# Attention and two feed-forward layers on one core: two score tiles in place of one, and late units' v product joined to later scores

## The chip, the cores and the metric

One core of one Trainium2 chip runs the whole program. The metric is the device time of one execution in microseconds, the median of several runs.

## What is computed

```python
def _attn_ref(q, k, v):                     # B, H, S, D = 4, 8, 576, 64
    scores = scale * np.matmul(q, k.transpose(0, 1, 3, 2))
    mask = block_i >= block_j               # blocks of 64 positions
    scores = np.where(mask, scores, -1000000000.0)
    attn = np.exp(scores - np.max(scores, axis=-1, keepdims=True))
    attn = attn / (np.sum(attn, axis=-1, keepdims=True) + 1e-09)
    return np.matmul(attn, v)
...                                         # heads side by side: x is 2304 x 512
    h = x @ w_in                            # 512 x 2048
    g = np.maximum(h, 0.0) + np.log1p(np.exp(-np.abs(h)))
    x = g @ w_out                           # 2048 x 512
...
    h = x @ w_in                            # second layer, 512 x 1024
    solu = h * softmax(h)
    out = (layer_norm(solu) * g_ln) @ w_out # 1024 x 512
```

Matrix products are made of float32 operands split in a high and a low part; a product is three matmuls.

## The kernel before

All work is recorded first as tasks in a `Plan`: an engine, a cost, the tasks it waits for, and a rank. The ranks are tables of numbers written at the top (`RANK` by group, `OFF` by kind of task). The planner makes from them one order for each engine, the kernel is emitted in that order, and each engine then runs its instructions in that order. Between engines the framework adds semaphore waits, by tile: it knows that a tile was written or read, and of neighbouring accesses of one engine to the same tile it signals the last.

The stages overlap. Their names here:

- **A units** (`UnitA`, n = 0 to 15): the first 256 queries of four batches, two heads at a time. Scores on TensorE (`mm_qk`), mask, maximum, scale and denominators on VectorE, exp on ScalarE, product with v (`pv`) on TensorE, then the rows of x (`x_hi`, `x_lo`) into `xt`. Units 8 to 15, the late ones, normalise on VectorE (`norm`), split (`split`), transpose by DMA (`tr_dma`), and `merge` into `psA`. Their scores take the PSUM tile `r`, from unit 12 on `r` and `R` in turn. `pv` writes into columns 0 to 255 of the unit's own tile, and the next unit on the same tile waits until `x_lo` has read it.
- **Pieces** (32): conversions of the first layer's weights, four steps on VectorE and one on ScalarE each, of 512 KB loads into `raw`; results are `w` and `w2w`.
- **Pairs** (72): 256 tokens and two 128-column slices of the first layer. On TensorE 24 matmuls `hp<-xt,w` (two *a blocks* of 12), then exp and ln on ScalarE, `t`, `gh`, `gl` on VectorE, and 24 matmuls `acc<-gh,w` and `acc<-gl,w` (two *b blocks* of 12). A chunk of tokens can start when its x is complete.
- **C units** (`UnitC`, 16): queries 256 to 575. TensorE: `mm_both` writes scores of blocks 0 (two heads, 384 columns) and 1 (two heads, 512 columns), 12 matmuls without a break; after a few a and b blocks the scores of block 2 (`mm_qk(2)`, 6 matmuls, written `S<-qkh` with 128x288 in the trace), which reuse the banks of block 0; and `pv` of the unit before (`S<-ps,v` and `S<-p,v`). VectorE: `mask` for blocks 0 and 1 (L467), `max` (L472) for 0, 1 and later 2. ScalarE: `exp` (L481), two heads of block 0 (`exp0`), two of block 1 (`exp1`), one instruction for block 2 (`exp2`). Then split, DMA transposes, merges into `ps` (L522), and `scale` (L538) and x from `pv`'s result.
- After the last C unit's x: the second layer, in which TensorE runs without gaps.

All four banks of a C unit's scores are one tile, `state["S"]` (L821): block 0 in banks 0 and 1, block 1 in banks 2 and 3, block 2 in banks 0 and 1 again, `pv` in bank 3 (`BANKS`, L76).

Of the kernel before, what the change touches and what calls it, by code (L numbers as in the profile page):

```python
# [10 lines left out]
F32 = mybir.dt.float32  # L11
# [12 lines left out]
    "Pair.a": -354.9, "Pair.abs": 39459.0, "Pair.b": 18236.7, "Pair.do_gh": 216226.0, "Pair.do_gl": 13257.7,  # L24
    "Pair.evac": -82948.2, "Pair.exp": -117702.0, "Pair.ln": -30665.3, "Pair.store": -79781.5, "Pair.stt": -62739.8,
    "Piece.bits0": -100434.0, "Piece.bits0@P0": -27714.9, "Piece.bits1": 65312.7, "Piece.bits1@P0": -101077.0,
    "Piece.do_hi": -19168.6, "Piece.do_hi@P0": -29991.6, "Piece.do_hi_g": -10835.1, "Piece.do_lo": 62401.8,
    "Piece.do_lo@P": -122217.0, "Piece.do_lo@P0": -16882.1, "Piece.do_lo_g": -33281.2, "Piece.load": 61438.7,
    "Piece.load@P0": -221951.0, "Piece.signed": -4876.1, "Piece.signed@P0": -103215.0, "Tok.a": -132718.0,
    "Tok.aggr": 7517.3, "Tok.bm": 58620.7, "Tok.center": -11408.7, "Tok.exp": -45235.8, "Tok.ln_hi": 28283.8,  # L30
    "Tok.ln_lo": 116041.0, "Tok.load": -268344.0, "Tok.logexp": -134098.0, "Tok.max": -65917.9,
    "Tok.merge": -135054.0, "Tok.mul": 52834.8, "Tok.o_evac": 47450.1, "Tok.small1": 71861.5, "Tok.small2": -55930.6,
    "Tok.split": -4685.6, "Tok.split_hi": 24778.5, "Tok.split_lo": -127140.0, "Tok.stats": 68934.5,
    "Tok.store": 157613.0, "Tok.tr": -45442.3, "Tok.x_hi": -107660.0, "Tok.x_lo": -20156.8, "UnitA.copy": -193390.0,
# [15 lines left out]
    "UnitC.den2": 65738.1, "UnitC.exp": 104667.0, "UnitC.load_qk": -83707.0, "UnitC.load_v": -36917.0,  # L50
    "UnitC.mask": -89564.7, "UnitC.max": -78960.5, "UnitC.merge": 54501.7, "UnitC.merge4": 149992.0,
    "UnitC.mm_both": -120396.0, "UnitC.mm_qk": -21356.3, "UnitC.norm": 76221.3, "UnitC.pv": -31503.3,
    "UnitC.qk_hi": -189467.0, "UnitC.qk_lo": -5389.2, "UnitC.rs_load": 138338.0, "UnitC.rs_store": -59470.7,
    "UnitC.scale": -44805.3, "UnitC.split": 94027.7, "UnitC.tr": -223984.0, "UnitC.x_hi": 131467.0,
    "UnitC.x_lo": 10651.6, "UnitC.xx": -154207.0,
}
RANK = {
# [3 lines left out]
    "Tok": (611105.0, 4133.14),  # L61
# [14 lines left out]
BANKS = (slice(0, 2), slice(2, 4), slice(0, 2))  # L76
# [139 lines left out]
def dve_ns(n, per=1.04):  # L216
    return 70.0 + per * n
# [11 lines left out]
def body(ctx: ExitStack, tc: tile.TileContext, qk, qkA, vP, vA, w1, w2, u1, u2, gln, out):  # L229
# [127 lines left out]
    class UnitC:  # L357
# [6 lines left out]
        def plan(self, prev, opened):  # L364
# [10 lines left out]
            for i, w in enumerate(WC):  # L375
# [10 lines left out]
                if i == 1 and p1:  # L386
                    p1.tail([self.t_exp[1, 1]])
# [58 lines left out]
        def scores(self, i):  # L446

            return state["S"][:, BANKS[i], 0:WC[i] if i < 2 else WC[2] // 2]

# [98 lines left out]
    class UnitA:  # L548
# [6 lines left out]
        def plan(self, prev, rank, opened):  # L555
# [14 lines left out]
            self.t_mqk = add("PE", 760, rank, self.mm_qk, [self.t_qk] + free)  # L570
# [127 lines left out]
        def x_hi(self, e):  # L698
            copy(e, xt_of(self.b)[:, 0, self.pr, :], self.o)
# [453 lines left out]
```

## Time and profile before

| | us |
|---|---|
| median of 3 runs | 783.55 |
| lowest, highest | 781.19, 784.84 |
| profiled execution, own time | 784.22 |
| its span on the core | 782.4 |
| TensorE busy | 735.1 (94%) |
| VectorE busy | 592.7 (76%) |
| ScalarE busy | 409.8 (52%) |

The span runs from the first to the last instruction; 1.8 us of the execution lie outside it. The page gives engines as PE (TensorE), PEld (its weight loads), DVE (VectorE), ACT (ScalarE), SP (which issues the DMAs). Idle time in brackets stands ahead of the instruction on whose line it is, with the instruction that ended it. PEclk is the granted TensorE clock, 1.00 being 2.4 GHz and 0.5 being 1.2 GHz; a stretch's figure is a mean.

### The profile page before, as it was taken

Reading aid. Unit: us, or ns where it says so; the run is one execution under the profiler, and the core shown is the slowest. Engines: PE = TensorE matmul, PEld = TensorE weight load, DVE = VectorE, ACT = ScalarE, POOL = GpSimd, SP = SyncE. Lnnn points to the kernel's source line nnn. Section 1 sums busy time; section 2 is a strip of 40 time slices with the busy share of each in tenths; the row PEclk is TensorE's granted clock in tenths of the full one; section 3 lists DMA queues with packets and bytes.
Section 4 is the critical chain, followed back from the end, with each engine's and each line's share of the span. In section 5 each row is a group of like instructions: output and inputs, shape, how many; then the busy total and the mean of one; then the engine's idle time right before and its main releaser. Section 6 shows DMA issues by size and latency. Waiting matters only on the chain.

```text
span 782.4 us, 13713 instructions
## 1 busy us (share of the span) xinstructions
PE 735.1 (94%) x5288; PEld 652.5 (83%) x5288; DVE 592.7 (76%) x1232; ACT 409.8 (52%) x877; POOL 0.7 (0%) x6
## 2 busy tenths in 40 slices
PE   7899999999898988898898899999999999999998
PEld 4688989999877777777887699999999888888887
DVE  6899995565777876777888755634698998989883
ACT  5787855563765666655665645543454342233231
POOL 0000000000000000000000000000000000000000
PEclk9899999999999998999999999999999999999999
DMA  7665742223666665566876552302513524443233
GB/s 258 197 196 182 227 149 68 69 42 88 138 135 148 138 165 123 116 132 134 172 148 132 101 138 81 124 13 72 200 52 82 141 76 108 95 108 88 59 83 80
DMA packets 165216, 95.00 MB, mean 121 GB/s; under 512 B 134816, under 2 KB 148384, under 8 KB 165152
## 3 DMA queue, kind: packets, MB, share of 16 engines
q1 hardware_dynamic: 165152, 94.14, 47.9%
q8 instruction: 41, 0.67, 0.3%
q14 instruction: 23, 0.19, 0.1%
HBM read 51.91 MB, written 9.70 MB: 79 GB/s over the span
## 4 chain that ended last, share of the span: by engine, by line
PE 64%; DVE 18%; ACT 10%; DMA 4%; issue 3%; SPq 0%; ACTq 0%; DVEq 0%
PE hp L238 14%; PE acc L238 13%; PE op L238 13%; PE h L238 13%; PE S L238 8%; ACT eC L481 5%; DVE mC L472 4%; DMA raw<-in_w_dram 3%; PE R L238 2%; DVE ps L522 2%; DVE a L315 1%; DVE t L769 1%; DVE mA L627 1%; PE r L238 1%; ACT eA L636 1%
## 5 line engine op out<-in xcount | busy, mean ns | idle before, releaser
L238 PE MATMUL hp<-xt,w 128*128 128x256 f32 x1728 | 216.6, 282 | 0.4 <-DVE t L769 0.3
L238 PEld LDWEIGHTS hp<-xt,w 128*128 128x128 f32 x1728 | 207.7, 190 | 6.9 <-issue 5.2
L238 PE MATMUL acc<-gh,w 128*128 128x256 f32 x768 | 144.8, 281 | 0.5 <-ACT gh L244 0.5
L238 PEld LDWEIGHTS acc<-gh,w 128*128 128x128 f32 x768 | 121.4, 189 | 3.0 <-issue 2.1
L238 PE MATMUL acc<-gl,w 128*128 128x256 f32 x384 | 107.6, 280 | 1.8 <-DVE gl L777 1.7
L238 PE MATMUL h<-u,w 128*128 128x512 f32 x432 | 100.2, 389 | 0.0
L238 PE MATMUL op<-w,w2w 128*128 128x512 f32 (+1 forms) x456 | 100.0, 378 | 0.0
L238 PEld LDWEIGHTS op<-w,w2w 128*128 128x128 f32 x456 | 82.5, 188 | 16.0
L238 PEld LDWEIGHTS h<-u,w 128*128 128x128 f32 x432 | 80.8, 188 | 16.6
L481 ACT ACTIVATE eC<-S,mC 128x384 f32<-128x384 f32 (+2 forms) x80 | 52.0, 653 | 61.0 <-DVE mC L472 26.9
L760 ACT ACTIVATE t<-hp 128x512 f32<-128x512 f32 x72 | 42.7, 593 | 66.1 <-PE hp L238 55.6
L769 DVE SCALAR_TENSOR_TENSOR t<-hp,t 128x512 f32<-128x512 f32 x72 | 49.1, 682 | 35.9 <-ACT t L766 35.5
L238 PEld LDWEIGHTS acc<-gl,w 128*128 128x128 f32 x384 | 72.1, 188 | 2.5 <-DVE gl L777 2.4
L238 PE MATMUL S<-ps,v 128*64 128x320 f32 (+1 forms) x256 | 38.8, 450 | 14.9 <-ACT eC L481 12.9
L1070 ACT ACTIVATE ob<-op,A 128x512 f32<-128x512 f32 (+1 forms) x19 | 12.6, 663 | 75.8 <-PE op L238 72.8
L777 DVE TENSOR_TENSOR gl<-t,gh 128x512 fp32r<-128x512 f32 x72 | 49.3, 684 | 2.0 <-ACT gh L244 0.7
L472 DVE TENSOR_REDUCE mC<-S 128x2 f32<-128x768 f32 (+2 forms) x48 | 45.4, 974 | 6.3 <-ACT eC L481 3.7
L238 PE MATMUL acc<-gh,w2w 128*128 128x256 f32 x256 | 48.4, 281 | 0.0
L766 ACT ACTIVATE t<-t 128x512 f32<-128x512 f32 x72 | 45.5, 632 | 1.4
L763 ACT ACTIVATE t<-t 128x512 f32<-128x512 f32 x72 | 45.6, 633 | 1.2
L522 DVE COPY ps<-eC 128x1536 uint16<-128x1536 uint16 (+2 forms) x48 | 45.2, 945 | 1.4 <-DMA eC<-hl 1.3
L238 PEld LDWEIGHTS S<-ps,v 128*64 128x64 f32 x256 | 18.5, 149 | 32.5 <-ACT eC L481 14.5
(175 smaller groups left out, 1086.0 us busy)
## 6 DMA issues: line engine op xcount, KB each, us to landing
raw<-in_w_dram SPq DMA_DIRECT2D x32, 512.0 KB, 4.7
qkC<-in_qk_dram SPq DMA_DIRECT2D x16, 480.0 KB
raw_u<-in_u_dram SPq DMA_DIRECT2D x11, 512.0 KB, 3.5
v<-in_vP_dram SPq DMA_DIRECT2D x16, 320.0 KB, 2.9
x2s<-stg SPq DMA_DIRECT2D x18, 256.0 KB, 2.8
xr<-x2s SPq DMA_DIRECT2D x18, 256.0 KB, 3.2
qkA<-in_qkA_dram SPq DMA_DIRECT2D x16, 256.0 KB, 4.0
out_dram<-ob SPq DMA_DIRECT2D x15, 256.0 KB, 2.2
```

The lines of the kernel that those rows point to most:

```text
L238: PE.matmul(out, lhsT, rhs, start=start, stop=stop, skip_group_check=True)
L315: DVE.scalar_tensor_tensor(out=self.a, in0=self.raw[:, :, 0], scalar=29, in1=self.a, op0=ALU.logical_shift_right, op1=ALU.bitwise_or)
L472: DVE.tensor_reduce(out=self.m[:, i:4:2] if i < 2 else self.m[:, 4:5], in_=self.scores(i), axis=AX.X if i < 2 else AX.XY, op=ALU.max, nega ...
L481: ACT.activation(e, sc, AF.Exp, bias=self.m[:, c:c + 1], accum_out=self.den[:, d:d + 1])
L522: DVE.tensor_copy(dst, src)
L627: DVE.tensor_reduce(out=self.m[:, i, w * j:w * j + w], in_=st[:, :, QA[i]], axis=AX.X, op=ALU.max, negate=True)
L760: ACT.activation(self.t, self.hp, AF.Abs)
L763: ACT.activation(self.t, self.t, AF.Exp, scale=-1.0)
L766: ACT.activation(self.t, self.t, AF.Ln, bias=1.0)
L769: DVE.scalar_tensor_tensor(out=self.t, in0=self.hp, scalar=0.0, in1=self.t, op0=ALU.max, op1=ALU.add)
L777: DVE.tensor_sub(self.gl, self.t, self.gh)
L1070: ACT.activation(self.ob[:, cols], self.o[cols.start][:, cols], AF.Copy, scale=self.A)
```

## The change

Three things change.

First, `state["S"]` becomes a list of two tiles of two banks. Blocks 0 and 2 go to the first, block 1 and `pv` to the second. The instructions of a C unit stay the same in kind and size. `pv` of the unit before is planned after the second `exp1` instead of the first.

Second, late A units all use `r`. Their `pv` writes 6 matmuls of 128 columns into columns 384 to 511 of both halves of `r`, where it was 4 matmuls of 256 and 128 columns into columns 0 to 255, so scores of a later unit and this product stand side by side. From unit 10 on one task (`mm_pv`) makes unit n's scores and, right behind, unit n-2's `pv`; units 14 and 15 get a `pv` of their own. Scores from unit 9 on wait for the exp of the unit before in place of the `x_lo`; `pv` waits for the `x_lo` of the unit before.

Third, every number of `OFF` and `RANK` is another.

```diff
 OFF = {
-    "Pair.a": -354.9, "Pair.abs": 39459.0, "Pair.b": 18236.7, "Pair.do_gh": 216226.0, "Pair.do_gl": 13257.7,
+    "Pair.a": -17732.7, "Pair.abs": -25663.4, "Pair.b": 30817.0, "Pair.do_gh": 252422.0, "Pair.do_gl": 4374.1,
...
-BANKS = (slice(0, 2), slice(2, 4), slice(0, 2))
...
-                    p1.tail([self.t_exp[1, 1]])
+                    p1.tail([self.t_exp[1, 0]])
...
-            return state["S"][:, BANKS[i], 0:WC[i] if i < 2 else WC[2] // 2]
+            return state["S"][i % 2][:, :, 0:WC[i] if i < 2 else WC[2] // 2]
...
-            o, ps = state["S"][:, 3], state["ps"]
+            o, ps = state["S"][1][:, 1], state["ps"]
...
-            self.bank = ("R", "r", "acc", "hp")[n] if n < 4 else "r" if n in (8, 9, 10, 11) else ("r", "R")[n % 2]
-            free = [u.t_xl for u in prev if u.bank == self.bank][-1:]
-            if n >= 12 and self.bank == "R":
-                free += evacs[1]
+            self.bank = ("R", "r", "acc", "hp")[n] if n < 4 else "r" if n >= 8 else ("r", "R")[n % 2]
+            free = [u.t_xl for u in prev if u.bank == self.bank][-1:] if n < 9 else [p1.t_exp]
...
-            self.t_mqk = add("PE", 760, rank, self.mm_qk, [self.t_qk] + free)
+            if n >= 10:
+                self.t_mqk = p2.tail(add("PE", 760 + 760, rank, partial(self.mm_pv, p2), [self.t_qk] + free + p2.pv_deps()))
+            else:
+                self.t_mqk = add("PE", 760, rank, self.mm_qk, [self.t_qk] + free)
...
+        def pv_deps(self):
+            return [self.t_cp, self.t_v] + ([self.p1.t_xl] if self.n > 8 else [])
...
+        def mm_pv(self, p2):
+            self.mm_qk()
+            p2.pv()
+
         def pv(self):
+            if self.n >= 8:
+
+                self.o = state["r"][:, :, 384:512]
+                for x, t in ((0, 0), (1, 0), (1, 1)):
+                    for j in range(2):
+                        mm(self.o[64 * j:64 * j + 64, x], self.v[:, j, t, :], self.ps[:, j, 128 * (x + t):128 * (x + t) + 128], t == 0, x == t)
+                return
...
-        state["S"] = q.tile([128, 4, 512], F32, name="S")
+        state["S"] = [q.tile([128, 2, 512], F32, name=f"S{i}") for i in range(2)]
...
+    for n in (14, 15):
+        plan.at_group("A3", n % 4)
+        unitsA[n].tail(add("PE", 760, 0.0, unitsA[n].pv, unitsA[n].pv_deps()))
```

What moves on the engines is shown at four places. ScalarE in a late C unit, before (eC_2322, eC_2323 and eC_2324 are blocks 0, 1 and 2, hl their splits; `waits` names the engines waited for):

```order
448 L481 ACTIVATE eC_2322,dC_2318<-S,mC 128x384 [waits DMAHW4_49,DVE_49,PE_49]
449 L766 ACTIVATE t<-t 128x512 [waits Activation_49]
450 L481 ACTIVATE eC_2322,dC_2318<-S,mC 128x384
451 L481 ACTIVATE eC_2323,dC_2318<-S,mC 128x512 [waits DMAHW5_49]
452 L244 ACTIVATE hl_2325<-eC_2322 128x768 [waits Activation_49]
453 L481 ACTIVATE eC_2323,dC_2318<-S,mC 128x512 [waits PE_49]
454 L430 ACTIVATE qkh<-qkC 128x384 [waits DMAHW7_49]
455 L431 ACTIVATE qkh<-qkC 128x576
456 L244 ACTIVATE hl_2326<-eC_2323 128x1024 [waits Activation_49]
457 L481 ACTIVATE eC_2324,dC_2318<-S,mC 128x576 [waits DMAHW0_49,DVE_49,PE_49]
458 L760 ACTIVATE t<-hp_131 128x512
```

And in the changed kernel, at the corresponding unit (S_2008 and S_2009 are the two tiles, eC_2016 to eC_2018 the blocks):

```order
435 L480 ACTIVATE eC_2016,dC_2012<-S_2008,mC 128x384 [waits DMAHW2_49,DVE_49,PE_49]
436 L480 ACTIVATE eC_2016,dC_2012<-S_2008,mC 128x384
437 L480 ACTIVATE eC_2017,dC_2012<-S_2009,mC 128x512 [waits DMAHW3_49,DVE_49,PE_49]
438 L786 ACTIVATE t<-hp_131 128x512 [waits PE_49,Activation_49]
439 L480 ACTIVATE eC_2017,dC_2012<-S_2009,mC 128x512
440 L789 ACTIVATE t<-t 128x512 [waits Activation_49]
441 L429 ACTIVATE qkh<-qkC 128x384 [waits DMAHW4_49,PE_49]
442 L430 ACTIVATE qkh<-qkC 128x576
443 L792 ACTIVATE t<-t 128x512 [waits Activation_49]
444 L480 ACTIVATE eC_2018,dC_2012<-S_2008,mC 128x576 [waits DVE_49]
```

The order of the five exps is the same, but which one waits for TensorE is not: the second exp of block 1 and the exp of block 2 did, where the change has waits at the first exp of each tile, and none on TensorE at block 2.

TensorE at two late A units (qkA scores, vA the product, r and R the PSUM tiles), before:

```order
414 L238 MATMUL r<-psA,vA 64x256 x2
415 L238 MATMUL r<-psA,vA 64x128 x2
416 L238 MATMUL hp_131<-xt,w_7_104 128x256 x12
417 L238 MATMUL hp_130<-xt,w_8_105 128x256 x12
418 L238 MATMUL r<-qkA 128x128 x2
419 L238 MATMUL r<-qkA 128x256 x2
420 L238 MATMUL R<-psA,vA 64x256 x2
421 L238 MATMUL R<-psA,vA 64x128 x2
422 L238 MATMUL hp_130<-xt,w_9_106 128x256 x12
```

And after the change, where scores of a unit are followed at once by the product of the unit two before:

```order
300 L237 MATMUL hp_131<-xt,w_10_107 128x256 x12
301 L237 MATMUL hp_131<-xt,w_11_108 128x256 x12
302 L237 MATMUL r<-qkA 128x128 x2
303 L237 MATMUL r<-qkA 128x256 x2
304 L237 MATMUL r<-psA,vA 64x128 x6
305 L237 MATMUL hp_130<-xt,w_12_109 128x256 x12
306 L237 MATMUL hp_130<-xt,w_13_110 128x256 x12
307 L237 MATMUL hp_131<-xt,w_14_111 128x256 x12
```

The products stood alone, with their own wait for `psA`; now a scores task carries them, and all are in `r`.

VectorE where the last piece of `w2w` is made, before (a and w2w belong to pieces, mA, dA, eA and psA to late A units, t, gh, gl to pairs):

```order
234 L315 SCALAR_TENSOR_TENSOR a<-raw,a 128x512
235 L246 CAST w2w_126<-a 128x512
236 L325 TENSOR_TENSOR w2w_126<-a,w2w_126 128x512
237 L703 TENSOR_TENSOR xt<-r,xt 128x256
238 L769 SCALAR_TENSOR_TENSOR t<-hp_130,t 128x512
239 L246 CAST gh<-t 128x512
240 L777 TENSOR_TENSOR gl<-t,gh 128x512
241 L622 MEMSET r 64x4x64
242 L627 TENSOR_REDUCE mA<-r 128x2 x2
243 L769 SCALAR_TENSOR_TENSOR t<-hp_131,t 128x512
244 L630 TENSOR_SCALAR mA<-mA 128x4
```

And after the change:

```order
264 L652 TENSOR_SCALAR dA<-dA 128x4
265 L324 TENSOR_TENSOR w2w_126<-a,w2w_126 128x512
266 L655 RECIPROCAL dA<-dA 128x4
267 L660 TENSOR_SCALAR eA_147<-eA_147,dA 128x128 x2
268 L660 TENSOR_SCALAR eA_147<-eA_147,dA 128x256 x2
269 L245 COPY eA_149<-eA_147 128x768 x2
270 L795 SCALAR_TENSOR_TENSOR t<-hp_130,t 128x512
271 L245 CAST gh<-t 128x512
272 L803 TENSOR_TENSOR gl<-t,gh 128x512
273 L634 MEMSET r 64x4x64
274 L245 CAST xt<-r 128x256
275 L639 TENSOR_REDUCE mA<-r 128x2
```

Five late units still have their mask (MEMSET of r or R) and maxima behind the last piece before, two after the change: three more late units are ahead of it. In TensorE's order the first blocks that use each piece keep nearly the same place (w_15 behind 48 blocks of 12 matmuls, the second half of w2w behind 56, in both). The first `mm_both` of the C units stands behind 94 blocks before, 72 after the change; between it and the last `pv` stand 110 blocks before, 118 after.

SP, which issues the loads in this order, at the start before (qkA and vA are A units' inputs, raw the pieces'):

```order
1 L599 DMA qkA<-in_qkA_dram 128x512
2 L603 DMA vA<-in_vA_dram 128x256
3 L599 DMA qkA<-in_qkA_dram 128x512
4 L603 DMA vA<-in_vA_dram 128x256
5 L304 DMA raw<-in_w_dram 128x1024
6 L599 DMA qkA<-in_qkA_dram 128x512
7 L603 DMA vA<-in_vA_dram 128x256
8 L304 DMA raw<-in_w_dram 128x1024 x3
9 L599 DMA qkA<-in_qkA_dram 128x512
```

And after the change:

```order
1 L611 DMA qkA<-in_qkA_dram 128x512
2 L615 DMA vA<-in_vA_dram 128x256
3 L303 DMA raw<-in_w_dram 128x1024
4 L611 DMA qkA<-in_qkA_dram 128x512
5 L615 DMA vA<-in_vA_dram 128x256
6 L303 DMA raw<-in_w_dram 128x1024 x3
7 L611 DMA qkA<-in_qkA_dram 128x512
8 L615 DMA vA<-in_vA_dram 128x256
9 L611 DMA qkA<-in_qkA_dram 128x512
```

Four loads of raw now stand ahead of the third unit's qkA, where one did; raw has a limited number of buffers, and a load that has to wait for one holds those behind it.

## Rows read from the trace of the kernel before

**Rows 1.** The page, part 1: busy us, share of the span, instructions.

```profile
PE 735.1 (94%) x5288; PEld 652.5 (83%) x5288; DVE 592.7 (76%) x1232; ACT 409.8 (52%) x877; POOL 0.7 (0%) x6
```

**Rows 2.** Busy time by stretch: its length, then each engine; then PEclk, DMA.

```profile
34.00:116.00 82.00, 77.72 (x670) 72.75 (x672) 79.23 (x177) 61.31 (x135) 0.00 (x0) 1.00 0.61 193
180.00:464.00 284.00, 254.09 (x2001) 220.88 (x2000) 214.39 (x439) 170.16 (x373) 0.00 (x0) 0.97 0.62 135
280.00:300.00 20.00, 15.65 (x116) 14.20 (x112) 14.81 (x30) 13.23 (x30) 0.00 (x0) 0.87 0.65 148
```

**Rows 3.** Waits, 180 to 464 us: who for what, total, times, longest.

```profile
PE S L238 <- ACT eC L481: 27.5, 17, 4.0
ACT eC L481 <- DVE mC L472: 26.9, 17, 4.9
...
PE S L238 <- DVE mC L472: 1.9, 4, 1.1
```

**Rows 4.** TensorE timeline, C stage: start, us, operation, [idle before <-releaser].

```profile
199.27 0.53 PE L238 MATMUL S<-qkh 128*128 128x288 f32 x2 [1.41 <-ACT eC L481]
...
296.01 0.85 PE L238 MATMUL S<-qkh 128*128 128x288 f32 x2 [4.00 <-ACT eC L481]
...
312.62 0.53 PE L238 MATMUL S<-qkh 128*128 128x288 f32 x2 [0.47 <-ACT eC L481]
...
404.09 2.88 PE L238 MATMUL hp<-xt,w 128*128 128x256 f32 x24
...
415.17 0.53 PE L238 MATMUL S<-qkh 128*128 128x288 f32 x2 [2.34 <-ACT eC L481]
...
417.89 2.16 PE L238 MATMUL S<-ps,v 128*64 128x320 f32 x16 [0.28 <-DVE mC L472]
...
448.79 2.16 PE L238 MATMUL S<-ps,v 128*64 128x320 f32 x16 [1.59 <-ACT eC L481]
```

**Rows 5.** ScalarE timeline of the unit at 407 to 424 us.

```profile
412.70 0.58 ACT L481 ACTIVATE eC<-S,mC 128x384 f32<-128x384 f32 x1 [1.29 <-DVE mC L472]
...
416.26 0.69 ACT L481 ACTIVATE eC<-S,mC 128x512 f32<-128x512 f32 x1 [0.41 <-PE S L238]
...
420.45 0.74 ACT L481 ACTIVATE eC<-S,mC 128x576 f32<-128x576 f32 x1 [1.48 <-PE S L238]
```

**Rows 6.** VectorE timeline of the same unit.

```profile
410.53 2.09 DVE L472 TENSOR_REDUCE mC<-S 128x2 f32<-128x768 f32 x2
...
417.07 0.76 DVE L472 TENSOR_REDUCE mC<-S 128x1 f32<-128x576 f32 x1 [0.45 <-ACT eC L481]
```

**Rows 7.** Groups by shape, VectorE, 180-464 us: busy, mean ns | idle.

```profile
L472 DVE TENSOR_REDUCE mC<-S 128x2 f32<-128x1024 f32 x16 | 19.4, 1212 | 0.0
```

**Rows 8.** Groups by shape, VectorE, 34 to 130 us.

```profile
L627 DVE TENSOR_REDUCE mA<-r 128x2 f32<-128x512 f32 x5 | 3.4, 676 | 0.0
L246 DVE CAST w<-a 128x512 fp32r<-128x512 f32 x8 | 3.3, 415 | 0.1
...
L661 DVE COPY psA<-eA 128x1536 uint16<-128x1536 uint16 x3 | 2.9, 956 | 0.6 <-DMA eA<-eA 0.6
...
L648 DVE TENSOR_SCALAR eA<-eA,dA 128x256 f32<-128x256 f32 x8 | 2.4, 347 | 0.0
L627 DVE TENSOR_REDUCE mA<-r 128x2 f32<-128x256 f32 x5 | 2.0, 397 | 0.0
L648 DVE TENSOR_SCALAR eA<-eA,dA 128x128 f32<-128x128 f32 x8 | 1.9, 282 | 0.1
...
L703 DVE TENSOR_TENSOR xt<-r,xt 128x256 fp32r<-128x256 f32 x3 | 1.2, 416 | 0.0
```

**Rows 9.** Timelines, VectorE and TensorE, where the last pieces are made and used.

```profile
114.76 0.68 DVE L325 TENSOR_TENSOR w<-a,w 128x512 fp32r<-128x512 f32 x1
...
116.25 5.92 PE L238 MATMUL hp<-xt,w 128*128 128x256 f32 x48
```

**Rows 10.** TensorE timeline at the start: the third unit's scores.

```profile
8.88 1.65 PE L238 MATMUL acc<-qkA 64*128 64x128 f32 x8 [1.49 <-DMA qkA<-in_qkA_dram]
```

More of the change, by code (lines that the diff above doesn't have):

```diff
@@ L29 @@
[L29 to L33, printed above, removed]
@@ L34 @@
-    "Tok.store": 157613.0, "Tok.tr": -45442.3, "Tok.x_hi": -107660.0, "Tok.x_lo": -20156.8, "UnitA.copy": -193390.0,
[15 rows of a table removed]
[L50 to L53, printed above, removed]
@@ L54 @@
-    "UnitC.scale": -44805.3, "UnitC.split": 94027.7, "UnitC.tr": -223984.0, "UnitC.x_hi": 131467.0,
-    "UnitC.x_lo": 10651.6, "UnitC.xx": -154207.0,
+    "Pair.a": -17732.7, "Pair.abs": -25663.4, "Pair.b": 30817.0, "Pair.do_gh": 252422.0, "Pair.do_gl": 4374.1,
+    "Pair.evac": 13972.5, "Pair.exp": -152676.0, "Pair.ln": -15664.0, "Pair.store": -94678.5, "Pair.stt": -68815.3,
+    "Piece.bits0": -175582.0, "Piece.bits0@P0": 2619.6, "Piece.bits1": 37851.8, "Piece.bits1@P0": -39422.8,
+    "Piece.do_hi": -21264.6, "Piece.do_hi@P0": -48361.9, "Piece.do_hi_g": 23570.6, "Piece.do_lo": 132424.0,
@@ new lines @@
+    "Piece.do_lo@P": -144568.0, "Piece.do_lo@P0": -50056.3, "Piece.do_lo_g": 73990.3, "Piece.load": 56483.4,
+    "Piece.load@P0": -232077.0, "Piece.signed": 56815.8, "Piece.signed@P0": -161172.0, "Tok.a": -245001.0,
+    "Tok.aggr": -46126.2, "Tok.bm": 60592.7, "Tok.center": -116996.0, "Tok.exp": -147154.0, "Tok.ln_hi": 14661.6,
+    "Tok.ln_lo": 202547.0, "Tok.load": -341930.0, "Tok.logexp": -176099.0, "Tok.max": -12029.7,
+    "Tok.merge": -143746.0, "Tok.mul": 79458.6, "Tok.o_evac": -8139.3, "Tok.small1": 75530.4, "Tok.small2": -23043.9,
@@ new lines @@
+    "Tok.split": 13453.5, "Tok.split_hi": -29626.1, "Tok.split_lo": -139011.0, "Tok.stats": 62413.2,
+    "Tok.store": 177190.0, "Tok.tr": -172324.0, "Tok.x_hi": -140171.0, "Tok.x_lo": -71993.7, "UnitA.copy": -225757.0,
[16 rows of a table added]
+    "UnitC.load_qk": -67717.5, "UnitC.load_v": -29311.6, "UnitC.mask": -115852.0, "UnitC.max": -181990.0,
+    "UnitC.merge": 14665.4, "UnitC.merge4": 199932.0, "UnitC.mm_both": -131363.0, "UnitC.mm_qk": -28198.2,
+    "UnitC.norm": -34567.8, "UnitC.pv": -46526.9, "UnitC.qk_hi": -334304.0, "UnitC.qk_lo": 65918.2,
@@ L56 @@
+    "UnitC.rs_load": 64973.1, "UnitC.rs_store": -123295.0, "UnitC.scale": 58365.4, "UnitC.split": 82733.6,
+    "UnitC.tr": -277333.0, "UnitC.x_hi": 141301.0, "UnitC.x_lo": 108011.0, "UnitC.xx": -199808.0,
 }
 RANK = {
[3 rows of a table removed]
-    "Tok": (611105.0, 4133.14),
[3 rows of a table added]
+    "Tok": (314401.0, 2050.55),
 }
@@ L587, in plan, with tail @@
                 t = add({"ACT": 264, "DVE": 335}, None, rank, self.copy_r, [t])
-            self.t_pv = add("PE", 718, rank, self.pv, [self.t_cp, self.t_v])
+            self.p1, self.group = p1, plan.group
+            prev.append(self)
             if n < 8:
-                t = add("DVE", 335, rank, self.scale_x, [self.t_pv, t])
-            self.t_xh = add({"ACT": 264, "DVE": 200 if n < 8 else 335}, None, rank, self.x_hi, [t if n < 8 else self.t_pv] + xfree(self.b))
-            self.t_xl = add("DVE", dve_ns(NA), rank, self.x_lo, [self.t_xh])
+                self.tail(add("PE", 718, rank, self.pv, self.pv_deps()), t)
+        def pv_deps(self):
+            return [self.t_cp, self.t_v] + ([self.p1.t_xl] if self.n > 8 else [])
+        def tail(self, pv, spread=None):
+            group, plan.group = plan.group, self.group
+            self.t_pv = t = pv
+            if self.n < 8:
+                t = add("DVE", 335, 0.0, self.scale_x, [pv, spread])
+            self.t_xh = add({"ACT": 264, "DVE": 200 if self.n < 8 else 335}, None, 0.0, self.x_hi, [t] + xfree(self.b))
+            self.t_xl = add("DVE", dve_ns(NA), 0.0, self.x_lo, [self.t_xh])
             xparts.setdefault(self.b, []).append(self.t_xl)
-            prev.append(self)
+            plan.group = group
+            return pv
         def load_qk(self):
@@ L698, in x_hi, with wide @@
         def x_hi(self, e):
-            copy(e, xt_of(self.b)[:, 0, self.pr, :], self.o)
+            copy(e, self.wide(xt_of(self.b)[:, 0, self.pr, :]), self.o)
         def x_lo(self):
             x = xt[self.b]
-            DVE.tensor_sub(x[:, 1, self.pr, :], self.o, x[:, 0, self.pr, :])
+            DVE.tensor_sub(self.wide(x[:, 1, self.pr, :]), self.o, self.wide(x[:, 0, self.pr, :]))
+        def wide(self, x):
+            return x if self.n < 8 else x.rearrange("p (a b) -> p a b", a=2)
     xparts = {}
```

6 lines of the change are left out of this document (1 added, 5 removed), and 37 rows, old and new, of tables (OFF, RANK).

## The prediction

> **What bounds the kernel now.** I read the engine table first: TensorE is busy 735.1 us of a span of 782.4 [rows 1], so no more than some 47 us can be won from its gaps, and the change leaves its matmuls as they are. The next view is busy time by stretch, where to look for the gaps. From 180 to 464 us, the C units, TensorE is busy 254.1 of 284 us: 29.9 us of the 47 lie here, and the granted clock is 0.97, so a part ran at 1.2 GHz [rows 2]. With f the share at half clock, 1 - f/2 = 0.97 gives f = 0.06, 17 us, which cost 8.5 us if TensorE was busy in all of it. What is winnable in this stage is thus 30 to 38 us. While the pieces are made, from 34 to 116 us, TensorE is idle 4.3 us and VectorE is busy 79.2 of 82: that stage has no room on VectorE.
>
> The waits of the C stage say why TensorE stops: 27.5 of its 29.9 idle us are waits for an exp, 17 times, 4.0 at most; 1.9 are waits for a maximum; and ScalarE's exps in turn wait 26.9 us for the maxima [rows 3]. The timeline of TensorE shows where: the scores of block 2, or pv when that stands first, come to the front of the queue 0.47 to 4.00 us before the exp that frees their bank is done [rows 4]. The two timelines of the unit at 407 us show what the exp waits for. The maxima of blocks 0 and 1 run back to back, 410.53 to 412.62, and exp0 starts at 412.70, after both, though it reads block 0 alone [rows 5, 6]. The four banks are one tile, and VectorE's accesses to it are signalled together. The same tile makes two more such waits there: exp2 starts at 420.45, after pv's matmuls, though the maximum it needs was done at 417.83 [rows 5, 6], and pv starts just after that maximum, with 0.28 us of idle time, though it doesn't use it [rows 4].
>
> The Trainium skill, "PSUM — Partial Sum Buffer", section "PSUM bank collisions raise a hardware error", asks for a guard between engines by bank and quadrant, simply by bank. By that rule exp0 and the maximum of block 1, in other banks, may run at once; no run here shows such a pair, since the tile's waits keep them apart. By that rule the first term below stands in full; if the two engines held each other up, it would be nothing.
>
> **The change part by part.** *Two tiles, exp0.* exp0 no longer waits for the maximum of block 1, 1.21 us by the mean of 16 [rows 7]. VectorE's order keeps both masks ahead of both maxima, so nothing more than that is taken off. A wait of TensorE for an exp then shrinks by 1.21 us, or goes if it was shorter. Six of the 17 are shorter, the least 0.47, and make 4.5 us together; the eleven others, the first of 1.41, the last of 1.59 and the longest of 4.00 among them, are over 1.21 [rows 4]. Gain: 11 x 1.21 + 4.5 = 17.8, with 9.7 of the 27.5 left. Bounds: 20.6 if each were cut in full, and 0 if something else holds exp0 (third rival). I take 17.8, because in this view the exp starts 0.08 us after the second maximum, so nothing else was later.
>
> *Two tiles, exp2 and pv.* exp2 no longer waits for pv: 420.45 - 417.83 = 2.6 us earlier in a unit of this order [rows 5, 6]. What it frees is used by the next unit's scores, some blocks later, so I count it at nothing; the blocks between hide it. pv no longer waits for the maximum of block 2: the 1.9 us of that wait go [rows 3]. pv is now planned behind the second exp1 rather than the first; that is one exp of 0.69 us [rows 5]. It falls behind the scores of block 2 and mostly a further block, so I take nothing; if that cover were gone it would be up to 16 x 0.69 = 11 us, the upper bound.
>
> *Number of blocks between.* 118 blocks of 12 matmuls lie in the stage instead of 110. One takes 1.4 us (24 in 404.09 to 406.90) [rows 4]. The work itself is not new, it comes out of the stages around, but 8 more blocks, 11 us, are cover for 16 units' waits. A shift of single blocks between units works both ways; I take nothing, and let it be part of why 9.7 us left is not too few.
>
> *Clock.* Of the longest waits, the one of 4.00 is followed by a pair of matmuls that takes 0.85 us where it otherwise takes 0.53, and the 20 us around it have a clock of 0.87 [rows 2, 4]. After 2.34 us the pair took 0.53 still. If the waits over 2 shrink to about 1, part of the 8.5 us comes back. Bounds 0 and 8.5; I take 2, because the largest wait keeps 2.8 us after the cut.
>
> *Late units and pieces.* By VectorE's order, three more late units have their masks and maxima ahead of the last pieces. Counted by kind, what is more in front of the last piece is 3 masks, 3 x (0.676 + 0.397) of maxima, 4 x 0.347 + 4 x 0.282 of normalising, 2 merges of 0.956, 2 x 0.416 for x, and 4 casts of w of 0.415 that ScalarE did before [rows 8]: 3.2 + 2.5 + 1.9 + 0.8 + 1.7 is 10.1 without masks and small ones, of which some 0.06 an instruction overlaps, so 9 to 10 us. About 2 of it stands behind the piece w_15, the one that matters: it ends at 115.4 and is used by the second of the a blocks that start at 116.25, so at 117.7 [rows 9], with 2.2 us to spare, while TensorE's own order keeps it behind 48 blocks in both kernels. So 7.5 - 2.2 = 5 us of TensorE waits if VectorE has no idle time to give, and about 2.5 if it gives the 2.8 of that stretch [rows 2]. I take 4; bounds 0 and 10. The product in six matmuls of 128 columns instead of four is the same 768 columns; I take nothing for it, and at most 8 units x 2 matmuls x 0.3 = 5 us if each costs like a whole one of a block.
>
> *Start.* Four loads of raw stand ahead of the third unit's inputs where one did. Its scores started at 8.88 us [rows 10], waiting for their load. If the fourth load waits for a free buffer, these scores come some 4 us later; the first a block needs four units, and these have slack among each other. I take 0; bounds -2 and +4.
>
> **Sum**, on the profiled execution of 784.2: -17.8 - 1.9 - 2 + 4 + 0 = 766.5. The median of the runs is 0.7 below that execution, so 765.8; I give 766.
>
> **The rivals.** *VectorE takes the place of the false wait.* In the unit shown the maxima start at 410.53, 3.6 us after the a blocks in front of mm_both ended [rows 4, 6], because VectorE had other work. With the stage shorter, VectorE is busy 214.4 of about 262 us, 82% instead of 75%. If half of what exp0 gains is lost to a later maximum, 8.9 us: 784.2 - 8.9 - 1.9 + 4 = 777.4, 777 by the median. For it: an in-order queue with merges of 1.2 us in it. Against: exp0 was late by VectorE's own maxima, not by other engines.
>
> *Clock back to full.* If no wait is long enough for a fall, the whole 8.5 comes back: 784.2 - 17.8 - 1.9 - 8.5 + 4 = 760.0, 759 by the median. For it: most of the waits over 2 us become about 1. Against: the 4.00.
> The Trainium skill, "TensorE: Matmul & The Clock Gate", section "HAM oscillation — how this bites in real kernels", says that waits between bursts send the clock to half; by that rule fewer waits give back all of it. The wait of 4.00 with 0.85 behind it agrees, the 2.34 with 0.53 doesn't decide.
>
> *Nothing gained.* The loop that sets the pace could be merge, maximum of block 1, exp1, split, transpose, merge, which the change doesn't shorten: then only 1.9 goes and the pieces cost 4: 786.3, 786 by the median. Against: TensorE's waits are put down to exps, not to merges.
>
> *Slower: the joined product.* TensorE now meets a late unit's product at the back of another unit's scores, six times joined and twice alone. If VectorE, 97% busy then, hasn't made psA of the unit two before, TensorE stands, and with it the pieces' users. It decides where the eight cost more than the 21.7 won in the C stage, 2.7 us each; with 4 us each, 784.2 - 21.7 + 4 + 32 = 798.5, and about 790 with 3. Against: two units' spacing is some 15 blocks, 21 us by 1.4 each, and a unit's VectorE work is about 5 us [rows 8].
>
> **How the numbers follow.** Chances: forecast 0.47, VectorE 0.19, full clock 0.12, nothing gained 0.09, joined product 0.13. Half a per cent, 3.9 us, is about what a measurement of this kernel can tell from no change. Faster takes the first three, 0.78; same is nothing gained, 0.09; slower 0.13. The range: from 754 (full clock, and the pieces cost nothing) to 785; it leaves out the slower case and small tails, under 2 in 10.
>
> **What would show it.** Right: exp0 starts after the first maximum, about 1 us into the second; TensorE's waits for an exp in the C stage near 10 us; TensorE's idle time from 34 to 116 us up by about 4; no waits of exp2 for pv. Wrong: maxima that start later after mm_both than now (VectorE rival); waits of several us in front of the joined scores or the products behind them (slower); waits for exp that stay at 27 us although exp0 starts earlier (nothing gained).

## The result and the profile after

The changed kernel takes 745.32 us, median of 6 runs (739.89 to 746.36), against 782.52 for the kernel before in the same runs: 0.9512 of its time, 95% interval 0.948 to 0.9544. It is faster by 37 us by the medians, and by 4.9% by the ratio. The forecast was 766 with a range down to 754; the time lies 9 us below it. The sign, and the place of the gain, were right; its size was not. The runs below come from several chips, on which the kernel before took 782.5 to 785.0 us as a median, so differences of 1 or 2 us between two runs say little.

The page of the changed kernel, the engine table and the chain of work that ended last by engine:

```profile
PE 724.3 (97%) x5320; PEld 647.5 (87%) x5320; DVE 594.8 (80%) x1244; ACT 401.7 (54%) x865; POOL 0.7 (0%) x6
...
PE 76%; DVE 11%; DMA 7%; ACT 3%; issue 2%; SPq 1%; DVEq 0%; ACTq 0%
```

TensorE stood idle 47 us of the span before; now 19. Its busy time fell as well, by 10.8 us with 32 matmul instructions more [rows 1]; the granted clock is 1.00 in every stretch now. Busy time by stretch, the pieces' stage and then the C units, which now stretch from 159 to 404 us (columns as in [rows 2]):

```profile
34.00:116.00 82.00, 79.14 (x692) 72.80 (x689) 78.32 (x189) 63.89 (x150) 0.00 (x0) 1.00 0.69 201
159.00:404.00 245.00, 243.78 (x1994) 215.85 (x1994) 210.14 (x433) 166.41 (x369) 0.00 (x0) 1.00 0.73 151
```

The C units hold TensorE for 245 us, with 1.2 us idle and the clock at 1.00, where 29.9 us were idle and the clock was 0.97 [rows 2]. The pieces' stage has 2.9 us idle, where it had 4.3. The waits in the C stage of the changed kernel:

```profile
ACT eC L480 <- DVE mC L471: 7.7, 7, 2.9
...
PE S L237 <- ACT eC L480: 1.1, 3, 0.5
```

TensorE waits 1.1 us for an exp, in three places, where it waited 27.5 in 17; ScalarE's wait for the maxima has gone from 26.9 to 7.7 [rows 3]. One late unit of the changed kernel, VectorE, then ScalarE, then TensorE, over the same 14 us (start, duration, operation):

```profile
368.82 2.07 DVE L471 TENSOR_REDUCE mC<-S 128x2 f32<-128x768 f32 x2
...
373.77 0.75 DVE L471 TENSOR_REDUCE mC<-S 128x1 f32<-128x576 f32 x1
...
376.97 0.49 DVE L537 TENSOR_TENSOR rC<-S,rC 128x320 f32<-128x320 f32 x1 [0.40 <-PE S L237]
```

```profile
369.83 0.58 ACT L480 ACTIVATE eC<-S,mC 128x384 f32<-128x384 f32 x1 [0.75 <-issue]
...
372.38 0.68 ACT L480 ACTIVATE eC<-S,mC 128x512 f32<-128x512 f32 x1
...
375.09 0.72 ACT L480 ACTIVATE eC<-S,mC 128x576 f32<-128x576 f32 x1
```

```profile
366.50 0.44 PE L237 MATMUL S<-qkh 64*128 64x384 f32 x2
...
372.13 0.43 PE L237 MATMUL S<-qkh 128*128 128x288 f32 x2
...
374.41 2.16 PE L237 MATMUL S<-ps,v 128*64 128x320 f32 x16
376.50 0.43 PE L237 MATMUL S<-p,v 128*128 128x64 f32 x2
```

mm_both starts at 366.50. In the unit before it started here, on TensorE:

```profile
406.90 0.45 PE L238 MATMUL S<-qkh 64*128 64x384 f32 x2
```

So the exp of block 0 came 5.80 us after mm_both's start (412.70 [rows 5]) and comes 3.33 us after it now. The two maxima still run back to back from 368.82, 2.07 us long. The exp of block 0 starts at 369.83, in the middle of them, where it started at their end [rows 5, 6]. The scores of block 2 start at 372.13 without a wait, where they waited 2.34 us [rows 4], and the exp of block 2 at 375.09, while pv runs (374.41 to 376.93), where it came after pv [rows 5].

A maximum and an exp now read two pairs of PSUM banks at once, and neither got longer: 2.07 us for the two maxima against 2.09, 0.58 for the first exp against 0.58 [rows 5, 6]. The Trainium skill, "PSUM — Partial Sum Buffer", section "PSUM bank collisions raise a hardware error", asks for a guard between engines by bank and quadrant, or simply by bank; the trace agrees, since the two ran at once in different banks.

### The profile page after: what moved, and what is told of

It is laid out like the page before. It is cut to its first block, busy times and chain, and to the rows that moved or that the text cites. A ratio compares the mean times of both kernels' runs of the same rounds, so it can differ in the third digit from the quotient of the medians.

```text
span 743.1 us, 13786 instructions
## 1 busy us (share of the span) xinstructions
PE 724.3 (97%) x5320; PEld 647.5 (87%) x5320; DVE 594.8 (80%) x1244; ACT 401.7 (54%) x865; POOL 0.7 (0%) x6
## 4 chain that ended last, share of the span: by engine, by line
PE 76%; DVE 11%; DMA 7%; ACT 3%; issue 2%; SPq 1%; DVEq 0%; ACTq 0%
PE hp L237 19%; PE acc L237 18%; PE op L237 13%; PE h L237 13%; PE S L237 8%; DMA eC<-hl 3%; PE R L237 2%; DMA eA<-eA 1%; DMA raw<-in_w_dram 1%; PE r L237 1%; ACT eC L480 1%; DVE mA L639 1%; DVE a L314 1%; DVE ps L521 1%; DVE gl L803 1%
## 5 line engine op out<-in xcount | busy, mean ns | idle before, releaser
L480 ACT ACTIVATE eC<-S,mC 128x384 f32<-128x384 f32 (+2 forms) x80 | 52.1, 654 | 22.5 <-issue 14.7
L237 PEld LDWEIGHTS acc<-gh,w2w 128*128 128x128 f32 x256 | 40.2, 189 | 0.8 <-issue 0.7
L243 ACT ACTIVATE hl<-eC 128x1024 uint16<-128x1024 uint16 (+2 forms) x42 | 36.4, 888 | 0.4
```

The lines of the kernel that those rows point to most:

```text
L237: PE.matmul(out, lhsT, rhs, start=start, stop=stop, skip_group_check=True)
L243: ACT.activation(out, a, AF.Copy)
L480: ACT.activation(e, sc, AF.Exp, bias=self.m[:, c:c + 1], accum_out=self.den[:, d:d + 1])
```

## The experiments

### Which part of the change: two tiles alone, and all but two tiles

two_tiles is the kernel before with this edit; every engine's order stays the same.

```diff
...
-            return state["S"][:, BANKS[i], 0:WC[i] if i < 2 else WC[2] // 2]
+            return state["S"][i % 2][:, :, 0:WC[i] if i < 2 else WC[2] // 2]
...
-            o, ps = state["S"][:, 3], state["ps"]
+            o, ps = state["S"][1][:, 1], state["ps"]
...
-            DVE.tensor_mul(self.xn, state["S"][:, 3, 0:NB], self.r)
+            DVE.tensor_mul(self.xn, state["S"][1][:, 1, 0:NB], self.r)
...
-        state["S"] = q.tile([128, 4, 512], F32, name="S")
+        state["S"] = [q.tile([128, 2, 512], F32, name=f"S{i}") for i in range(2)]
```

> The kernel before with one edit: the scores of a C unit in two tiles of two banks. Tables, late units and with them every engine's order stay. If the tile's waits are the main cause (theory A), the exp of block 0 starts 1.0 to 1.3 us earlier after mm_both, TensorE's waits for an exp fall from 27.5 to below 10 us, the clock comes back with them, and 20 to 30 of the 37 us come: 753 to 763. If it is the new order that brings VectorE to the masks earlier (theory B), the gain stays under 15: 768 to 775, and the masks start as late as before, 2.9 us after mm_both starts.

Measured: 744.92 us, ratio 0.9512 (0.9473 to 0.955). All of the gain, and more than theory A expected. TensorE's busy time, and its stretches for the pieces and the C units, in two_tiles:

```profile
PE 725.0 (98%) x5288; PEld 647.3 (87%) x5288; DVE 589.9 (79%) x1232; ACT 408.9 (55%) x877; POOL 0.7 (0%) x6
```

```profile
34.00:116.00 82.00, 78.09 (x676) 73.21 (x673) 79.01 (x177) 61.60 (x136) 0.00 (x0) 1.00 0.65 195
192.00:426.00 234.00, 233.30 (x1912) 205.56 (x1911) 206.61 (x428) 164.99 (x367) 0.00 (x0) 1.00 0.76 162
```

The same 110 blocks and 16 units that took TensorE from 191.9 to 464 us before now take it from 192.7 to 425: 40 us less. 29.2 of them are idle time (29.9 to 0.7), and TensorE's busy time over the whole kernel is 10.1 us lower for the same instructions [rows 1]. Most of that is the clock, which is 1.00 in this stretch: the 17 us that this stage spent at half clock before explain up to 8.5 us; the rest was not taken apart. The pieces' stage is as it was.

one_tile is the changed kernel with the reverse edit: one tile of four banks, everything else as changed.

> The changed kernel with one edit undone: the scores of a C unit are one tile of four banks again; order, tables and late units are those of the changed kernel. Theory A: exp of block 0 waits for both maxima again, 1.1 us later, waits for an exp return to 15 to 25 us and half-clock stretches come back: 765 to 778. Theory B: the new order hides the tile's waits: under 757.

Measured: 785.11 us, ratio 1.0023 (0.9991 to 1.0056), so all of the gain is gone. TensorE waits for an exp as long in all, and as often, as in the kernel before:

```profile
PE S L239 <- ACT eC L482: 27.5, 17, 3.1
```

Theory A stands, and B, that the new order brings VectorE to the masks earlier, falls. The masks do start earlier, 2.15 us after mm_both's start in two_tiles against 2.95 before as means of 16 units; but the order there is the old one. Waits that go elsewhere let VectorE arrive earlier by itself. The exp of block 0 follows: as means of the same 16 units it starts 5.57 us after mm_both before, and 3.52 us after it in two_tiles.

### The other two parts, alone and together

new_tables is the kernel before with the changed kernel's OFF and RANK; late_only the kernel before with the new late units and nothing else; old_tables the changed kernel with the old OFF and RANK; old_late the changed kernel with the old late units.

> The kernel before with the numbers of OFF and RANK of the changed kernel alone. Theory A: the exps still wait for both maxima, so the C stage loses 25 us or more: 770 to 790. Theory B: masks start about 0.8 us earlier and the time falls by 10 to 20 us: 763 to 773.

Measured: 797.15 us, ratio 1.0184 (1.0138 to 1.023): slower by 13 us, more than either theory had; what it lost was not taken apart.

> The kernel before with the late units' change alone: all in one bank pair, product joined to the scores of the next but one; old numbers, one tile of scores. The first mm_both stands behind 70 blocks instead of 94. The prediction's term (4 us more waiting while the pieces are made) gives 785 to 792; if the joined product costs nothing and the earlier C stage is only moved, 778 to 785.

Measured: 794.14 us, ratio 1.013 (1.0079 to 1.0181): slower by 10, beyond what either expectation had. The pieces' stage of late_only, and of old_tables below it:

```profile
34.00:116.00 82.00, 73.44 (x636) 66.64 (x635) 78.62 (x196) 59.48 (x149) 0.00 (x0) 0.96 0.69 196
```

```profile
34.00:116.00 82.00, 73.40 (x635) 66.63 (x635) 78.54 (x196) 59.17 (x148) 0.00 (x0) 0.96 0.68 194
```

TensorE is idle 8.6 us of these 82, against 4.3 before [rows 2], and the granted clock is 0.96. The 4.3 us more have the place and the size of the prediction's term, but the cause is another. TensorE's two largest sums of waits in this stretch of late_only:

```profile
PE acc L239 <- DVE gh L247: 3.4, 1, 3.4
PE acc L239 <- DVE gl L805: 2.4, 5, 1.0
```

They are for a pair's gh and gl, which VectorE made late while it worked on late units and pieces; no wait there is for a piece, which is what the prediction had worked the term out from. So the size is luck.

> The changed kernel with the numbers of OFF and RANK of the kernel before: two tiles and the new late units. If costs add (late_only was 10 us slower than the kernel before): 753 to 757. If those 10 us came from the C stage, which two tiles relieve, and only the pieces' stage lost: 748 to 752.

Measured: 755.96 us, ratio 0.9659 (0.9636 to 0.9682). The costs add: 11 us above two_tiles.

> The changed kernel with the late units as before: two tiles and the new numbers. If the numbers were made for the new late units and cost without them what they cost alone (13 us): 753 to 760. If that cost was in the C stage: 745 to 750.

Measured: 749.1 us, ratio 0.9561 (0.9532 to 0.9589), 4 us above two_tiles: most of the 13 that the new numbers cost with one tile is gone with its waits.

| two tiles | late units | numbers | us |
|---|---|---|---|
| no | no | old | 783 to 785 |
| no | new | old | 794.1 |
| no | no | new | 797.2 |
| no | new | new | 785.1 |
| yes | no | old | 744.9 |
| yes | new | old | 756.0 |
| yes | no | new | 749.1 |
| yes | new | new | 745.3 |

Two tiles are worth 38 to 48 us in all four pairs. The late units cost 10 and 11 us with the old numbers and gain 12 and 4 with the new ones; the new numbers cost 13 and 4 us with the old late units and gain 9 and 11 with the new. They belong together, and together they are worth nothing that can be measured, with either kind of tile.

### Which waits of the one tile

The next kernels start from two_tiles and put single waits back, by reordering or by small instructions that need the result waited for.

max_swap: block 1's maximum ahead of block 0's.

```diff
-            DVE.tensor_reduce(out=self.m[:, i:4:2] if i < 2 else self.m[:, 4:5], in_=self.scores(i), ...)
+            for i in ((1, 0), (), (2,))[i]:
+                DVE.tensor_reduce(out=self.m[:, i:4:2] if i < 2 else self.m[:, 4:5], in_=self.scores(i), ...)
```

> two_tiles with the two maxima of a unit in the other order: block 1 first, then block 0, so that the exp of block 0 again starts after both (1.2 us later) and every other wait stays away. The theory of the prediction (this one wait is nearly all) gives back most of the 39 us: 768 to 782. The theory that the false waits act together, the exp of block 2 held by pv as much as this one, gives 750 to 762.

Measured: 755.35 us, ratio 0.9643 (0.962 to 0.9665), 10.4 us above two_tiles. So the wait that the prediction took for nearly all of the gain is a quarter of it by itself.

exp2_waits: the exp of block 2 behind pv.

```diff
+            if i == 2 and self.p1 and state.get("pv of") is self.p1:
+                copy("ACT", self.t([128, 64], "scr", 1), state["S"][1][:, 1, 0:64])
             e, sc = state["eC"][i][:, j, :], self.scores(i)
...
+            state["pv of"] = self
```

> two_tiles with a small ScalarE copy (64 columns of pv's output) ahead of the exp of block 2, so that this exp again waits for pv where pv is emitted first; the copy itself costs ScalarE some 0.2 us a unit. The prediction counted this wait at nothing: 745 to 748. If it keeps ScalarE, the splits behind it and so the next unit late, 753 to 765.

Measured: 747.76 us, ratio 0.9544 (0.9521 to 0.9567), 2.8 us above two_tiles. The prediction's nothing is nearly right for this wait by itself.

both_waits has both edits.

> two_tiles with both edits: maxima swapped, and the copy ahead of the exp of block 2. If these two waits are all of what the one tile cost: 778 to 788. If the others of the one tile (the mask waiting for all 12 matmuls, pv for the maximum of block 2, the maximum of block 2 for the exps of block 1) count as well: under 772.

Measured: 766.69 us, ratio 0.9788 (0.9767 to 0.9808), 21.8 us above two_tiles. Together they cost 8.6 us more than the sum of the two, 13.2. Where these 8.6 lie is shown behind three_waits.

Where the rest was came out of the trace of the kernel before. ScalarE's first exp of block 1 in the unit at 407 us [rows 4 to 6]:

```profile
413.79 0.57 ACT L481 ACTIVATE eC<-S,mC 128x384 f32<-128x384 f32 x1
...
414.35 0.68 ACT L481 ACTIVATE eC<-S,mC 128x512 f32<-128x512 f32 x1
```

It ends at 415.03, and TensorE starts the scores of block 2 at 415.17 [rows 4], 0.14 us later. These scores reuse the banks of block 0 and need its exps alone, the second of which ended at 414.36. ScalarE's exps of one unit stand close to each other, and with one tile TensorE waited for the last of them that was ahead. Of the nine units in which these scores stand ahead of pv, seven waited for an exp of block 1.

scores2_wait puts this one back.

```diff
             S, w = self.scores(i), WC[i]
+            if i == 2:
+                mm(S[:, 0, 0:2], ident, self.den[:, 1:5:3], True, True)
```

> two_tiles with one small matmul (identity by two columns of the exps' sums, some 0.1 us) ahead of each unit's scores of block 2, so that these scores again wait for the exp of block 1 that stands ahead of them, as 7 of the 9 units with this order did in the kernel before (they started 0.14 us after such an exp ended, not after the exp of block 0). If that was the wait that my sum took for one on block 0: 752 to 760, by itself. If with the exp 1.9 us earlier TensorE has its blocks as cover even so: 745 to 749.

Measured: 750.46 us, ratio 0.9577 (0.9549 to 0.9605). 5.5 us above two_tiles, of which 2.8 are the added matmuls themselves (TensorE busy 727.8 against 725.0).

three_waits has all three.

> two_tiles with all three waits put back: maxima swapped, the exp of block 2 behind pv, the scores of block 2 behind the exps of block 1. If these are what the one tile cost: 778 to 788. If more of it sits in the remaining ones (pv for the maximum of block 2, that maximum for the exps of block 1): 768 to 776.

Measured: 775.82 us, ratio 0.9905 (0.9871 to 0.9939), 30.9 above two_tiles, or 28 without the added matmuls; by the expectation, more sits in the waits that are left. The engine tables of max_swap, exp2_waits, scores2_wait, both_waits and three_waits, in this order:

```profile
PE 725.6 (96%) x5288; PEld 646.9 (86%) x5288; DVE 592.7 (79%) x1232; ACT 407.9 (54%) x877; POOL 0.7 (0%) x6
...
PE 723.7 (97%) x5288; PEld 646.4 (87%) x5288; DVE 589.6 (79%) x1232; ACT 410.6 (55%) x892; POOL 0.7 (0%) x6
...
PE 727.8 (97%) x5320; PEld 650.5 (87%) x5320; DVE 590.4 (79%) x1232; ACT 409.3 (55%) x877; POOL 0.7 (0%) x6
...
PE 732.0 (96%) x5288; PEld 650.2 (85%) x5288; DVE 592.4 (77%) x1232; ACT 410.7 (54%) x892; POOL 0.7 (0%) x6
...
PE 736.5 (95%) x5320; PEld 655.4 (85%) x5320; DVE 592.7 (77%) x1232; ACT 411.6 (53%) x892; POOL 0.7 (0%) x6
```

With the span of each profiled execution they give TensorE's idle time, the span less the busy time. Against two_tiles (span 743.4, busy 725.0, idle 18.4):

| run | span | more idle | more busy | PEclk, 190 to 480 us |
|---|---|---|---|---|
| max_swap | 754.7 | 10.7 | 0.6 | 1.00 |
| exp2_waits | 745.9 | 3.8 | -1.3 | 1.00 |
| scores2_wait | 748.1 | 1.9 | 2.8 | 1.00 |
| both_waits | 765.1 | 14.7 | 7.0 | 0.98 |
| three_waits | 773.1 | 18.2 | 11.5 | 0.98 |

The idle time nearly adds up: 14.5 singly against 14.7 for two waits, 16.4 against 18.2 for three. What the single runs don't have is the added busy time: but for the small matmuls the work is the same, and the clock is below 1.00. So the waits are worth more together mainly because TensorE then runs a part of the stage at 1.2 GHz. An estimate: a PEclk of 0.98 over 290 us is some 12 us at half clock and costs half of that, 6 us of the 7.0 in both_waits, and of the 8.7 in three_waits that its added matmuls don't account for; the rest is open.

Three more were put back on top of three_waits, one after the other: four_waits, a small matmul on the maximum of block 2 ahead of pv; five_waits, also a ScalarE copy of block 2's scores ahead of an exp of block 1 that follows them; six_waits, also the masks swapped, so that both wait for all of mm_both.

> three_waits with a fourth wait put back: a small matmul on the maximum of block 2 ahead of pv in the eight units where that maximum stands ahead, so that pv waits for it as in the kernel before. The small matmuls themselves cost TensorE about 0.17 us each (scores2_wait was busy 2.8 us more than two_tiles in 16), here 4 us in all. If this wait carries the rest: 782 to 790. If the rest is in none of the four: 776 to 779.

> four_waits with a fifth wait put back: a small ScalarE copy (64 columns of block 2's scores) ahead of each exp of block 1 that is emitted behind the scores of block 2, so that this exp waits for those scores, as the exp at 416.26 us did in the kernel before (idle 0.41, released by TensorE). If this holds ScalarE, and with it the splits and VectorE: 779 to 787. If not: 773 to 776.

> five_waits with the two masks of a unit in the other order, so that VectorE waits for all 12 matmuls of mm_both before either mask, as it did with one tile. The masks of block 0 then start 0.3 to 0.4 us later in units where VectorE is free early. If that is the rest: 2 to 5 us above five_waits. If VectorE is late there anyway: within 1.5 us of it.

Measured: 773.29 (ratio 0.9879, 0.984 to 0.9917), 772.72 (0.9851, 0.9815 to 0.9887) and 773.01 us (0.9854, 0.982 to 0.9887). None of the three adds to the time; four_waits and five_waits came out below both of their expectations. Each is some 2.5 us below three_waits, with more work in it. By their pages that is TensorE's busy time (734.0, 731.2 and 732.1 us against 736.5) and not its idle time (37.2, 39.8 and 37.0 against 36.6), with a mean granted clock of 0.989 to 0.991 over the span, against 0.987. Why the clock fell less often is open.

The traces of before and of three_waits differ in one more wait. The scaling of pv's result on VectorE in a unit where the scores of block 2 follow pv at once; first TensorE and VectorE in the kernel before, then in three_waits:

```profile
401.60 0.43 PE L238 MATMUL S<-p,v 128*128 128x64 f32 x2
...
402.45 0.43 PE L238 MATMUL S<-qkh,qkl 128*128 128x288 f32 x2
...
402.92 0.49 DVE L538 TENSOR_TENSOR rC<-S,rC 128x320 f32<-128x320 f32 x1 [2.54 <-PE S L238]
```

```profile
393.51 0.43 PE L237 MATMUL S<-p,v 128*128 128x64 f32 x2
...
394.59 0.42 PE L237 MATMUL S<-qkh,qkl 128*128 128x288 f32 x2
...
393.98 0.49 DVE L543 TENSOR_TENSOR rC<-S,rC 128x320 f32<-128x320 f32 x1 [1.68 <-PE S L237]
```

Before, the scaling started 0.04 us after the end of the scores (402.45 + 0.43), though pv had ended at 402.03, and VectorE stood 2.54 us; in three_waits it starts 0.04 us after pv. scale_waits is three_waits with this put back, in the seven units of this order.

```diff
+                self.q2 = self.p1 and state.get("pv of") is self.p1
...
             self.xn = self.r
+            if state["cur"].q2:
+                DVE.tensor_copy(self.t([128, 64], "scd", 1), state["S"][0][:, 1, 0:64])
```

> three_waits with one more wait put back: a small VectorE copy ahead of the scaling of pv's result in the seven units where the scores of block 2 follow pv at once, so that this scaling waits for both, as it did with one tile (in the kernel before it started 1.1 us after pv's end there, at the end of the scores, and VectorE stood idle 14.2 us for it against 8.4 in three_waits). If VectorE's order behind it is the rest: 780 to 787. If not: 775 to 778.

Measured: 781.94 us, ratio 0.9984 (0.9968 to 1.0): the kernel before, to within 0.2%. TensorE's wait for an exp went from 19.7 us in three_waits, the first line, to 25.2, against 27.5 before:

```profile
PE S L237 <- ACT eC L485: 19.7, 14, 2.5
...
PE S L237 <- ACT eC L487: 25.2, 16, 2.5
```

Of its eight copies the one behind the last unit finds nothing to wait for; ahead of the seven others VectorE stands 14.1 us, as it stood 14.2 ahead of the scaling before. The masks start 2.94 us after mm_both as a mean, as late as before (2.95), where it is 2.55 in three_waits. About 3 us of the 782 are the added matmuls, so a few us of the 39 are still in something that was not put back.

| two_tiles and | us | above two_tiles |
|---|---|---|
| nothing | 744.9 | |
| exp of block 2 for pv | 747.8 | 2.8 |
| scores of block 2 for exps of block 1 | 750.5 | 5.5 |
| exp of block 0 for both maxima | 755.4 | 10.4 |
| the first and the third | 766.7 | 21.8 |
| all three | 775.8 | 30.9 |
| all three, and scaling for scores of block 2 | 781.9 | 37.0 |

## Why the prediction was wrong in size

**What held.** The C stage was the place, TensorE's waits for exps the loss, the one tile the cause, and the exp of block 0 starts inside the maxima. The waits of pv for a maximum are gone. Of the rivals, VectorE's later maxima and the loop through the merge did not come, and in the changed kernel no wait of TensorE stands at the joined products.

**The step that failed: each wait for an exp shrinks by 1.21 us, and 9.7 us are left.** All of the 27.5 went but 1.1. Two reasons, both read from the traces:

- The exp of block 0 was to gain the one maximum, since "nothing more than that is taken off". In two_tiles, with the same order, it starts 2.05 us earlier after mm_both (5.57 to 3.52): 1.04 us are the maximum, and most of the rest is that VectorE itself reaches the masks 0.80 us earlier. An estimate: 2.05 us off each of the 17 waits of the kernel before leaves 3.0 us of the 27.5. The prediction had not listed the wait that shows this best, the scaling's. In the lists of waits no matmul waits for it, but it held VectorE some 0.8 us in each of seven units (14.2 us of idle time before, 8.4 in three_waits); put back, it makes the masks late again and the kernel 6.1 us slower.
- The prediction took the exp that TensorE waited for to be the one that frees the bank. In seven of the nine units with the scores of block 2 first it was an exp of block 1, and this was a false wait too. The trace of before had it, in rows that the prediction did not show: 415.17 is 0.14 us behind the end of an exp of block 1.

**The second step: the clock.** I took 2 of 8.5 us, since one wait of 2.8 would remain. No wait for an exp over 0.55 us remained, the clock of the stage was 1.00, and TensorE's busy time fell by 10.8 us in the changed kernel, 10.1 in two_tiles. The rival "clock back to full" was right in what it said of the clock, and it alone would still have given only 759. The two steps hang together: put back one at a time, the false waits left the clock at 1.00; put back together, they didn't.

**The third: pieces and late units, +4.** In the changed kernel the term is not there: the pieces' stage has 1.4 us less idle time than before. late_only and old_tables have 4.3 us more, but through a pair's gh and gl and not through a piece. The prediction sized it from VectorE's order alone, and the new numbers take it back, by means that were not taken apart. A bound in the same part prices a matmul of a block at 0.3 us, where 24 in a row take 2.88 [rows 4], 0.12 each; nothing was taken for it, so the sum doesn't change.

In the sum, the gaps were to shrink by 17.8 and 1.9 and to grow by 4, 15.7 us in all, and the busy time by 2. TensorE's idle time fell by 28.5 us (47.3 to 18.8) and its busy time by 10.8: 784.2 less 39.3 is 744.9, and the profiled execution took 744.99.

## What to carry to other kernels

A PSUM tile that several engines take turns on should be no larger than what one step uses: here the split of one tile in two, with no instruction moved, was worth 5%. When a tile's waits are false, list all of them, for every engine that touches the tile, by what ended just before each instruction starts, before pricing any; a wait that starts 0.1 us after something it doesn't need is found that way. Don't price such waits by the time that each costs alone: here three cost 18.7 us singly and 30.9 together, the idle time nearly the same, the difference mainly in TensorE's clock, so they should be removed together in a run before the order is tuned further.

## What was not expected of the hardware

Where waits were long, the clock added to their cost. The C stage of max_swap, of both_waits and of one_tile (stretch, then busy time by engine, PEclk), the first two with TensorE's wait for exps (total, times, longest):

```profile
190.00:480.00 290.00, 279.40 (x2286) 250.04 (x2284) 233.73 (x473) 187.44 (x406) 0.00 (x0) 1.00 0.67 144
...
PE S L237 <- ACT eC L481: 10.3, 14, 1.8
```

```profile
190.00:480.00 290.00, 274.46 (x2198) 242.29 (x2198) 227.66 (x462) 183.06 (x410) 0.00 (x0) 0.98 0.65 140
...
PE S L237 <- ACT eC L483: 15.1, 15, 2.3
```

```profile
190.00:480.00 290.00, 258.12 (x2046) 228.24 (x2045) 210.68 (x424) 165.97 (x358) 0.00 (x0) 0.98 0.58 125
```

With waits of at most 1.8 us for an exp the granted clock stayed 1.00 in max_swap, though they sum to 10.3 us; with the longest at 2.3 in both_waits and 3.1 in one_tile it was 0.98, part of the stretch at 1.2 GHz. In both_waits TensorE starts again at 243.79, 320.90 and 414.25 us after waits of 2.31, 2.23 and 2.09 us, and the granted clock is 0.50 from 244 to 246, 322 to 325 and 415 to 417. Length alone doesn't decide: in the kernel before, the wait of 2.34 us that ended at 415.17 [rows 4] left the clock at 1.00 up to 420, and in one_tile one of 1.82 us that ended at 270.54 was followed by 0.50 from 272 to 275. What a wait costs is thus more than its length where the clock falls behind it. The Trainium skill, "TensorE: Matmul & The Clock Gate", section "HAM oscillation — how this bites in real kernels", says that waits between bursts bring the clock down; the trace agrees for the three waits over 2 us in both_waits and shows no fall for the many short ones of max_swap.
